# Longer transfer runs, another order for the first batch and narrower key sums in a sketched attention with a multiplicative FFN

## The chip, the core and the metric

The kernel runs on one core of one Trainium2 chip. A core has five engines that run side by side: TensorE (PE; its weight loads are shown as PEld), VectorE (DVE), ScalarE (ACT), GpSimd (POOL) and SyncE (SP), which here issues all transfers. The metric is the time of one execution in device microseconds.

## What is computed

Four batches, four heads, 1088 positions, head width 32. Queries and keys are sketched with two 8 x 32 matrices S1 and S2; the outer product of the two sketches is a feature vector of 64. Attention is linear in these features. Its output, as a 4352 x 128 matrix, goes through an FFN without a nonlinearity.

```python
def phi(x):
    a = np.einsum('rd,bhsd->bhsr', S1, x)
    b = np.einsum('rd,bhsd->bhsr', S2, x)
    return np.einsum('bhsi,bhsj->bhsij', a, b).reshape(*x.shape[:-1], r * r)
q_p, k_p = phi(q), phi(k)
kv = np.einsum('bhsf,bhsd->bhfd', k_p, v)
z = np.sum(k_p, axis=2)
num = np.einsum('bhsf,bhfd->bhsd', q_p, kv)
den = np.einsum('bhsf,bhf->bhs', q_p, z)[..., None] + 1e-06
x = (num / den)                    # then (B,H,S,D) -> (B*S, H*D)
a = x @ w1; b = x @ w2             # 4352 x 1024
out = ((a * b) @ w3) @ w_out       # 4352 x 128
```

q, k and v come as float32, S1, S2 and the weights as float64.

## The kernel before

**Layout.** A batch has 1024 "main" positions (128 partitions x 8 consecutive positions j) and a rest of 64; the rests of two batches share a tile. All four heads of a position lie side by side as 128 columns. `load_main` (L83-86) loads one tensor of one batch in four transfers, one per head, into a tile [128, 8, 4, 32]; the runs are one position of one head, 128 bytes.

**Keys** (`k_steps`, L408-479). `lead` (L389) rounds all of k to a coarse grid: k1 (bf16), the remainder k2 (DVE, L395) and ks = k + k1 (POOL, L396). For each half of four chunks of 128 positions, `k_feat` transposes k (L366), copies it (ACT, L368), multiplies it with the sketches (L375), copies one factor (L379) and forms the features kp (DVE, L383). Then `kvs` runs `gram` (L412) for each chunk: v' kp in two products, each for two heads (64 array columns, L415), k1' k1 (L418, bf16) and k2' ks (L419), both for all four heads at once (128 columns, of which the blocks of one head with itself are used). `fin1` to `fin4` (L439-478) add the rest, mask out the blocks, and turn the sums through two small chains of products into the operands Rh, Rf, Rl that the queries are multiplied with, and kz.

**Queries** (`q_steps`, L485-607), for each half of a batch: transposes (L498), a copy (L500), rounding on DVE into q1 and, with a subtraction on POOL (L508), q2; `ay`: for each chunk a bf16 product (L518) and two fp32 ones (L523, L525); then `split`, `dens` and `phi`, all DVE; transposes of the features (L584), a copy (L587), the product with kz (L602) and a copy to xT (L605), the FFN's input.

**FFN.** There are nine groups, eight of 512 positions (half a batch) and the rest of 256. In `ffn_ab` each group runs eight steps c: a (L646), a copy of a on ACT (L648), b (L650), and a*b on DVE (L652). w3 and w_out are multiplied on chip into w3o; `ffn_o` (L659) multiplies each a*b with it, LAG = 10 steps behind `ffn_ab`. `ffn_out` transposes and stores.

**Weights.** Each chunk of 128 x 512 float64 words arrives raw, up to NRAW = 6 at a time, and `convert` (L199-217) makes float32 of it with two ACT operations (L209, L210) and four of DVE (L212 to L216). There are 4 chunks of w1 and w2, 2 of w_out and 16 of w3; those of w3 are transposed (L327) and multiplied with w_out (L335).

**Order.** Each part is a list of steps with a cost; `merge` (L694) interleaves lists in proportion to their costs, and L712-726 write the stages down: first the keys and queries of batch 0 with the conversion of w1 and w2, then FFN group 0 with the next half of the queries and half of the remaining conversions, and so on. The framework's planner takes this order as a priority: where an engine would be idle by its own model, it puts in an instruction that comes later in the program but is ready. All transfers wait in SP's one queue in the order so planned.

## Time and profile before

| | us |
|---|---|
| median of three runs | 360.63 (360.4 to 361.77) |
| the profiled execution | 360.9 |
| its span | 359.1 |
| busy: PE, PEld, DVE, ACT, POOL | 309.2, 182.1, 207.1, 115.4, 22.3 |
| DMA packets (20.70 MB) | 58643, of which 53760 under 512 B |

The profile is of one execution. A row of a timeline or chain gives start and length in us, the engine, the line of the kernel, and the tile that is written; "x8" means that eight instructions are merged in the row. An fp32 product is two instructions, each with a weight load of its own. A group row gives the busy time, the mean of one instruction in ns, and the idle time in front of them. Windows give the busy time of each engine in a stretch. SPq is the issue of transfers on SP. The granted clock is the share of TensorE's full clock that its throttle passes on.

### The profile page before, as it was taken

The numbers are of one execution on the slowest core, as the hardware profiler recorded it, in microseconds if no ns is written. First come the engines' busy times: TensorE is split into PE (matmuls) and PEld (weight loads), VectorE is DVE, ScalarE is ACT, GpSimd is POOL, SyncE is SP. The second block draws the span as 40 slices with busy tenths as digits, with TensorE's granted clock in tenths as the row PEclk, the third lists the DMA queues.
The fourth block names the chain that finished last, engine by engine and source line by source line (L and its number), as shares of the span: only waits on it lengthen the run. The fifth ranks groups of instructions, "written<-read, shape, count | busy, mean of one in ns | idle before, by whom it ended". The sixth has DMA issues, their size and how long they took to land.

```text
span 359.1 us, 4019 instructions
## 1 busy us (share of the span) xinstructions
PE 309.2 (86%) x1404; PEld 182.1 (51%) x1404; DVE 207.1 (58%) x575; ACT 115.4 (32%) x211; POOL 22.3 (6%) x21
## 2 busy tenths in 40 slices
PE   2488224299999999999999999999999999999993
PEld 1354214237666766746554544655454454354652
DVE  6655977948994696637654573743348364362210
ACT  1144024245793323242222224130322422333311
POOL 0300021010000020001030101000010100000000
PEclk9995555559999999999999999999999999999998
DMA  7899699146300330012000000000000000000001
GB/s 102 143 320 130 132 187 379 55 70 226 117 0 2 58 60 1 0 24 37 31 0 0 0 33 0 0 31 0 0 2 29 1 0 31 0 29 0 3 28 44
DMA packets 58643, 20.70 MB, mean 58 GB/s; under 512 B 53760, under 2 KB 55040, under 8 KB 58624
## 3 DMA queue, kind: packets, MB, share of 16 engines
q1 hardware_dynamic: 58624, 20.46, 25.4%
q8 instruction: 11, 0.18, 0.2%
q14 instruction: 8, 0.07, 0.1%
HBM read 18.22 MB, written 2.23 MB: 57 GB/s over the span
## 4 chain that ended last, share of the span: by engine, by line
PE 80%; DVE 9%; SPq 3%; ACT 2%; DMA 2%; POOL 1%; issue 1%; DVEq 0%; POOLq 0%; ACTq 0%
PE ps_o L659 16%; PE a_ps L646 16%; PE b_ps L650 15%; PE ps_kvz L415 4%; PE ps_w3o L335 4%; PE ps_kvz L419 3%; PE ps_ay L523 3%; PE ps_x L602 3%; PE ps_ay L525 3%; PE ps_ph L584 2%; PE ps_ab L375 2%; SPq L85 2%; PE ps_wt L327 2%; PE ps_kvz L418 2%; DMA k_sb<-in_k_dram 2%; POOL q L508 1%
## 5 line engine op out<-in xcount | busy, mean ns | idle before, releaser
L652 DVE TENSOR_TENSOR ab<-ffa,b_ps 128x512 f32<-128x512 f32 (+1 forms) x72 | 47.2, 655 | 56.8 <-PE b_ps L650 52.8
L646 PE MATMUL a_ps<-xT,w 128*128 128x512 f32 (+1 forms) x144 | 72.6, 587 | 0.0
L650 PE MATMUL b_ps<-xT,w 128*128 128x512 f32 (+1 forms) x144 | 71.3, 577 | 0.0
L659 PE MATMUL ps_o<-ab,w3o 128*128 128x512 f32 (+1 forms) x144 | 69.4, 578 | 0.7 <-ACT ob L662 0.7
L648 ACT COPY ffa<-a_ps 128x512 f32<-128x512 f32 (+1 forms) x72 | 40.5, 562 | 82.9 <-PE a_ps L646 82.9
L650 PEld LDWEIGHTS b_ps<-xT,w 128*128 128x128 f32 x144 | 27.2, 193 | 28.2 <-issue 25.1
L659 PEld LDWEIGHTS ps_o<-ab,w3o 128*128 128x128 f32 x144 | 25.5, 190 | 24.7 <-issue 20.5
L646 PEld LDWEIGHTS a_ps<-xT,w 128*128 128x128 f32 x144 | 24.4, 195 | 14.9 <-issue 11.5
L508 POOL TENSOR_TENSOR q<-qT,q 128x512 f32<-128x512 f32 (+1 forms) x9 | 10.0, 1107 | 178.3 <-DVE q L232 178.3
L415 PE MATMUL ps_kvz<-kp,v_sb 128*64 128x128 f32 x128 | 16.2, 335 | 3.3 <-DVE kp L383 3.3
L419 PE MATMUL ps_kvz<-ks,k 128*128 128x128 f32 (+1 forms) x72 | 18.5, 344 | 0.0
L209 ACT ACTIVATE cv_c<-raw 128x512 f32<-128x512 f32 x22 | 14.7, 674 | 11.3 <-DVE cv_t L215 8.0
L523 PE MATMUL ps_ay<-Rf,q 128*128 128x64 f32 (+1 forms) x72 | 15.0, 301 | 3.4 <-POOL q L508 3.4
L224 DVE TENSOR_REDUCE g_q<-qT 128x1 f32<-128x512 f32 (+1 forms) x9 | 5.9, 657 | 20.0 <-ACT qT L500 20.0
L584 PE MATMUL ps_ph<-ident,ph 128*128 128x128 f32 x68 | 10.0, 290 | 8.7 <-DVE ph L577 8.7
L335 PEld LDWEIGHTS ps_w3o<-wo,w3T 128*128 128x128 f32 x128 | 15.6, 192 | 2.4 <-issue 2.4
L396 POOL TENSOR_TENSOR ks<-k_sb,k 128x1024 f32<-128x1024 f32 x4 | 10.6, 2651 | 95.2 <-DVE k L232 95.2
L335 PE MATMUL ps_w3o<-wo,w3T 128*128 128x128 f32 x128 | 16.3, 276 | 0.0
L215 DVE SCALAR_TENSOR_TENSOR cv_t<-cv_c,cv_t 128x512 int32<-128x512 int32 x22 | 15.8, 723 | 0.3
L210 ACT ACTIVATE cv_m<-raw 128x512 int32<-128x512 uint32 x22 | 14.7, 675 | 3.0 <-DVE w3c L216 2.6
L525 PE MATMUL ps_ay<-Rl,qT 128*128 128x96 f32 (+1 forms) x72 | 15.0, 302 | 0.0
L584 PEld LDWEIGHTS ps_ph<-ident,ph 128*128 128x128 f32 x68 | 8.6, 150 | 12.6 <-issue 12.3
(156 smaller groups left out, 386.9 us busy)
## 6 DMA issues: line engine op xcount, KB each, us to landing
raw<-in_moe_w_dram SPq DMA_DIRECT2D x20, 512.0 KB, 5.3
k_sb<-in_k_dram SPq DMA_DIRECT2D x16, 128.0 KB, 3.8
v_sb<-in_v_dram SPq DMA_DIRECT2D x16, 128.0 KB, 4.0
q_sb<-in_q_dram SPq DMA_DIRECT2D x16, 128.0 KB, 3.4
out_dram<-oT SPq DMA_DIRECT2D x8, 256.0 KB, 2.1
raw<-in_moe_w_out_dram SPq DMA_DIRECT2D x2, 512.0 KB, 9.1
kr<-in_k_dram SPq DMA_DIRECT2D x4, 32.0 KB, 2.3
vr<-in_v_dram SPq DMA_DIRECT2D x4, 32.0 KB, 2.3
```

The lines of the kernel that those rows point to most:

```text
L215: nc.vector.scalar_tensor_tensor(t, ci, -(1 << 31), t, ALU.bitwise_and, ALU.bitwise_or)
L335: nc.tensor.matmul(ps, t[:, c], wo[:, c], start=(c == 0), stop=(c == NC - 1))
L415: nc.tensor.matmul(acc["kv"][64 * p:64 * (p + 1)], vt[rows, 2 * p:2 * p + 2].rearrange("p h d -> p (h d)"), kp_chunk[rows, 2 * p:2 * p + 2 ...
L419: nc.tensor.matmul(acc["g2"], k2[rows], ks[rows], start=False, stop=last, skip_group_check=True)
L523: nc.tensor.matmul(C[rows, j, :64], s["q2"][:, cols], Rf[:, b].rearrange("p x h i -> p (x h i)"), start=True, stop=False, skip_group_check ...
L525: nc.tensor.matmul(C[rows, j], s["qT"][:, cols], Rl[:, b].rearrange("p x h i -> p (x h i)"), start=False, stop=True, skip_group_check=True)
L584: nc.tensor.transpose(ps[:, p, j * 128:(j + 1) * 128], s["ph"][:, j, 2 * p:2 * p + 2].rearrange("p h i j -> p (h i j)"), ident)
L646: nc.tensor.matmul(a_ps[:, :n], w1[:, cols], xT[key], start=True, stop=True)
L648: nc.scalar.copy(a_sb[:, :n], a_ps[:, :n])
L650: nc.tensor.matmul(b_ps[:, :n], w2[:, cols], xT[key], start=True, stop=True)
L652: nc.vector.tensor_mul(ab[:, :n], a_sb[:, :n], b_ps[:, :n])
L659: nc.tensor.matmul(o_ps[g][:, :n], w3o[:, c], ab_sb.pop((g, c))[:, :n], start=c == 0, stop=c == NC - 1)
```

## The change

1. **Transfers.** `load_main` becomes one transfer per tensor and batch, into a tile [128, 4, 8, 32]; a run is the eight positions of one head, 1 KB. The order "position, then head", which the transposes need, is made by a copy on ACT for each half (`natural`), for k and for q.
2. **First batch first.** The stage of batch 0 is an explicit order of steps instead of a merge: both halves' transposes and features come before the first sums; the query transposes and rounding come between the steps of the key chain; the four conversions of w1 and w2 are put at given places. The preparation of the sketches becomes three steps in it. The loads are issued k, its rest, v, q, then weights. For batch 0, ks is formed on DVE instead of POOL, and the keys use the three PSUM buffers of tag "h".
3. **Key sums** in products of one head each, 32 array columns: for each chunk four products v' kp with 64 moving columns, four k2' ks and four k1' k1 with 32 each. All v' kp of a half come first, then all k2' ks, then all k1' k1. What follows in `fin1` works on 128 x 32 instead of 128 x 128 and spreads the result over the blocks at the end.
4. **Last product later.** `ffn_o` runs 16 steps behind in groups 0 and 1, is then brought down to 4 behind in a stage of its own beside the first query half of batch 1, and stays 6 behind later and 2 in the last group.
5. **Smaller ones.** In `ay`, the bf16 products of all four chunks come first. `convert` uses the target as its scratch tile, and NRAW is 4. Four spreads of the sketches go from DVE to POOL. A one-element ACT copy is put at the start.

The core of the diff:

```diff
-LAG = 10
-NRAW = 6
+LAG = 16
+NRAW = 4
...
     def load_main(t, src, b):
-        for h in range(H):
-            nc.sync.dma_start(t[:, :, h], bass.AP(tensor=src.tensor, offset=(b * H + h) * S * D,
-                                                  ap=[[NJ * D, 128], [D, NJ], [1, D]]))
+        nc.sync.dma_start(t.rearrange("p h j d -> p h (j d)"),
+                          bass.AP(tensor=src.tensor, offset=b * H * S * D,
+                                  ap=[[NJ * D, 128], [S * D, H], [1, NJ * D]]))
...
+    def natural(t, half):
+        n = work.tile([128, 4, H, D], F32, tag="nat", name="nat")
+        nc.scalar.copy(n, bview(t[:, 0, 4 * half], [[D, 4], [NJ * D, H], [1, D]]))
+        return n.rearrange("p j h d -> p j (h d)")
...
-    load_k(0)
+    load_in("k", 0)
     load_rest(k_rs[0], k, 0)
+    load_in("v", 0)
+    load_in("q", 0)
     load_rest(v_rs[0], v, 0)
-    load_q(0)
     load_raw(NRAW)
...
-    def lead(kf, n, pool, name):
+    def lead(kf, pool, name, eng):
...
-        nc.gpsimd.tensor_add(ks, kf, k1)
+        def second():
+            nc.vector.tensor_sub(k2, kf, k1)
+            eng.tensor_add(ks, kf, k1)
...
-            for p in range(2):
-                nc.tensor.matmul(acc["kv"][64 * p:64 * (p + 1)], vt[rows, 2 * p:2 * p + 2].rearrange("p h d -> p (h d)"),
-                                 kp_chunk[rows, 2 * p:2 * p + 2].rearrange("s h i j -> s (h i j)"),
-                                 start=first, stop=last, skip_group_check=True)
-            nc.tensor.matmul(acc["g1"], k1[rows], k1[rows], start=False, stop=last, skip_group_check=True)
-            nc.tensor.matmul(acc["g2"], k2[rows], ks[rows], start=False, stop=last, skip_group_check=True)
+            def products(out, lhs, rhs, start):
+                for i, c in enumerate(chunks):
+                    for h in range(H):
+                        nc.tensor.matmul(out[h * D:(h + 1) * D], c[lhs][rows, h], c[rhs][rows, h],
+                                         start=start and i == 0, stop=last and i == len(chunks) - 1,
+                                         skip_group_check=True)
+            products(acc["kv"], "v", "kp", first)
+            products(acc["g2"], "k2", "ks", False)
+            products(acc["g1"], "k1", "k1", False)
...
-    run(merge(rest_steps(0) + k_steps(0) + q_main(0, 0), weight_steps(("w1", "w2"))))
-    w_st = weight_steps(("wo", "w3"))
-    cut = len(w_st) // 2
-    run(merge(ffn_steps(0), q_main(0, 1), w_st[:cut]))
-    run(merge(ffn_steps(1), k_steps(1) + q_main(1, 0), w_st[cut:]))
-    run(merge(ffn_steps(2), q_main(1, 1), rest_steps(1) + k_steps(2)))
...
+    w_in, w_out = weight_steps(("w1", "w2")), weight_steps(("wo", "w3"))
+    (ld1, ld2, tr0, ab0, kv0, tr1, ab1, kv1, *fins), r0, q00 = ([f for _, f in x] for x in (k_steps(0), rest_steps(0), q_main(0, 0)))
+    wi = [f for _, f in w_in]
+    for f in ([sketch_pairs, tr0, tr1, sketch_T, ld1, ab0, ld2, ab1] + r0 + [kv0, kv1, fins[0], sketch_P, q00[0], fins[1], q00[1],
+              wi[0], fins[2], fins[3], wi[1], q00[2], wi[2]] + q00[3:5] + [wi[3]] + q00[5:]):
+        f()
+    cut = len(w_out) * 2 // 5
+    run(merge(ffn_steps(0, 16), q_main(0, 1), w_out[:cut]))
+    run(merge(ffn_steps(1, 16), k_steps(1), w_out[cut:]))
+    run(merge(ffn_steps(None, 4), q_main(1, 0)))
+    run(merge(ffn_steps(2, 6), q_main(1, 1), rest_steps(1) + k_steps(2)))
...
```

In the explicit order, `q00[0]` are the query transposes, `q00[1]` their rounding, `q00[2]` the products, `q00[3:5]` `split` and `dens`, and `q00[5:]` the rest up to xT; `fins` are `fin1` to `fin4`, and `wi` the four conversions of w1 and w2.

More of the change, by code (lines that the diff above doesn't have):

```diff
@@ L410, in k_steps, with gram, ld1, chunk @@
         acc = {}
-        def gram(k1, k2, ks, kp_chunk, vt, rows, first, last):
-            k1, k2, ks = (x.rearrange("p h d -> p (h d)") for x in (k1, k2, ks))
-            for p in range(2):
-                nc.tensor.matmul(acc["kv"][64 * p:64 * (p + 1)], vt[rows, 2 * p:2 * p + 2].rearrange("p h d -> p (h d)"),
-                                 kp_chunk[rows, 2 * p:2 * p + 2].rearrange("s h i j -> s (h i j)"),
-                                 start=first, stop=last, skip_group_check=True)
-            nc.tensor.matmul(acc["g1"], k1[rows], k1[rows], start=False, stop=last, skip_group_check=True)
-            nc.tensor.matmul(acc["g2"], k2[rows], ks[rows], start=False, stop=last, skip_group_check=True)
-        def ld():
-            acc["k"] = lead(k_sb[b], NJ * HD, work, "")
-        st.append((1.0, ld))
+        def gram(chunks, rows, first, last):
+            def products(out, lhs, rhs, start):
[7 more added lines that the diff above has]
+            products(acc["g1"], "k1", "k1", False)
+        def ld1():
+            acc["k"], first, acc["second"] = lead(k_sb[b], work, "", nc.gpsimd if b else nc.vector)
+            first()
+        st += [(0.5, ld1), (0.5, lambda: acc["second"]())]
         for half in range(NJ // 4):
-            feat, state = k_feat(lambda j, half=half: k_sb[b][:, 4 * half + j].rearrange("p h d -> p (h d)"), 4, None)
+            def chunk(half=half):
+                n = natural(k_sb[b], half)
+                return [n[:, j] for j in range(4)]
+            feat, state = k_feat(chunk, 4, None, "t" if b else "h")
             st += feat
@@ L610, in srcs @@
         def srcs():
-            return [q_sb[b][:, 4 * half + j].rearrange("p h d -> p (h d)") for j in range(4)]
+            n = natural(q_sb[b], half)
+            return [n[:, j] for j in range(4)]
         def after():
             if half == 1 and b + 2 < B:
-                load_q(b + 2)
+                load_in("q", b + 2)
         return q_steps(srcs, (b, half), [[(b, 0, 128)]] * 4, after)
```

236 lines of the change are left out of this document (121 added, 115 removed).

## The prediction

> **What bounds the kernel now.** I read the windows first, cut at the places where the matrix engine's work changes: the first FFN product starts at 75.24 us, the last piece of w3 @ w_out and the second FFN group are done by 158.65, the last group's products end near 345.5.
>
> ```profile
> 0.00:75.24 75.24, 34.73 (x154) 24.88 (x155) 53.62 (x175) 21.74 (x38) 8.23 (x11) 0.69 0.82 173
> 75.24:158.65 83.41, 82.31 (x450) 53.35 (x450) 58.03 (x141) 37.41 (x70) 4.44 (x3) 0.97 0.25 58
> 158.65:345.50 186.85, 184.80 (x775) 99.33 (x774) 95.04 (x258) 54.12 (x99) 9.65 (x7) 1.00 0.05 13
> 345.50:359.10 13.60, 7.38 (x29) 4.52 (x28) 0.42 (x1) 2.10 (x5) 0.00 (x0) 0.90 0.10 29
> ```
>
> The columns are length, then busy time of PE, PEld, DVE, ACT and POOL, the granted clock, the DMA share and GB/s. From 75.24 to 345.50 PE is busy for 267.1 of 270.3 us: that part only gets shorter if PE gets less to do. Before 75.24 PE is busy for less than half, at a clock of 0.69 on average, and that part gets shorter if the chain of the first batch does. The chain of waits shows this chain (start, length, what; an excerpt without holes of its longest pieces):
>
> ```profile
> 13.63 1.13 PE ps_kt L366 x4
> 15.42 1.98 PE ps_ab L375 x8
> 17.73 1.24 DVE kp L383
> 27.75 1.15 DVE kp L383
> 40.78 1.14 DVE g_k L224
> 42.65 5.75 DMA k_sb<-in_k_dram
> 50.52 1.13 PE ps_qt L498 x4
> 54.29 1.21 POOL q L508
> 60.90 1.12 DVE g_k L224
> 68.42 1.95 PE ps_ph L584 x8
> 70.39 1.02 ACT pT L587
> 71.46 2.00 PE ps_x L602 x4
> 74.12 1.11 PE ps_qt L498 x4
> 75.24 1.71 PE a_ps L646 x2
> ```
>
> Three things stand out. The second half of the keys gets its features (27.75) ten microseconds after the first (17.73), because PE runs the first half's sums in between. Work of the next batch lies on the chain (g_k at 40.78 and 60.90, the k_sb transfer at 42.65), because the planner fills DVE with whatever is ready. And the queries are transposed at 50.52, when everything of the keys is done. The same windows over the two stretches in which DVE carries the chain, and DVE's largest groups in each (line, what | busy us, mean ns | idle):
>
> ```profile
> 36.00:49.60 13.60, 3.04 (x12) 2.78 (x12) 13.02 (x43) 0.00 (x0) 2.12 (x1) 0.50 0.85 157
> 59.79:75.24 15.45, 5.03 (x17) 2.98 (x18) 13.60 (x38) 5.30 (x8) 0.00 (x0) 0.50 0.28 113
> ```
>
> ```profile
> L395 DVE TENSOR_TENSOR k<-k_sb,k 128x1024 f32<-128x1024 f32 x1 | 2.9, 2894 | 0.0
> L216 DVE CUSTOM_DVE_ANT_0 wo<-cv_t,cv_m 128x1024 uint16<-128x1024 uint16 x2 | 1.4, 693 | 0.1
> L215 DVE SCALAR_TENSOR_TENSOR cv_t<-cv_c,cv_t 128x512 int32<-128x512 int32 x2 | 1.4, 680 | 0.0
> L224 DVE TENSOR_REDUCE g_k<-k_sb 128x1 f32<-128x1024 f32 x1 | 1.2, 1207 | 0.0
> ```
>
> ```profile
> L215 DVE SCALAR_TENSOR_TENSOR cv_t<-cv_c,cv_t 128x512 int32<-128x512 int32 x4 | 2.7, 684 | 0.0
> L212 DVE TENSOR_SCALAR cv_c<-cv_c 128x512 f32<-128x512 f32 x6 | 2.4, 422 | 1.6 <-ACT cv_c L209 1.6
> ```
>
> All of these rows are foreign to the first batch's chain: at least 6.9 us (2.9 + 1.4 + 1.4 + 1.2) in the first stretch and, with g_k's 1.12, at least 6.2 us (2.7 + 2.4 + 1.12) in the second.
>
> **Part 1: the first batch's chain.** I move five marks of the chain, before to after.
>
> *Mark 1, first transposes of the keys: 13.63.*
>
> ```profile
> 1.54 3.05 SPq L85 DMA_DIRECT2D k_sb<-in_k_dram  x4
> ```
>
> ```profile
> raw<-in_moe_w_dram SPq DMA_DIRECT2D x20, 512.0 KB, 5.3
> k_sb<-in_k_dram SPq DMA_DIRECT2D x16, 128.0 KB, 3.8
> ```
>
> The four pieces of k are issued from 1.54 to 4.59, and a piece lands 3.8 us after its issue; then the small rest rows go first on PE and DVE. After, one issue at 1.54 brings all 512 KB. A raw chunk is as large and lands in 5.3 us with longer runs and other transfers in front of it; that is the upper bound, a piece's 3.8 the lower: 5.3 to 6.8, I take 6.0, the middle. New is the reordering copy (natural, 128x512 on ACT). The kT copy has that shape, and with its hand-over lasts from 14.76 (13.63 + 1.13) to 15.42: 0.66. Mark 1 becomes 6.7. Sixteen such copies are 10.6 us of ACT, which is busy for 115 of 359; they need only landed data and two buffers, so the planner can put them early; if one is not, PE waits 0.66 us for it, at most 13 times, in the stall term below.
>
> *Mark 2, sums over the keys done.* Two rows of the key sums at the slow clock (the main chunk at 33.08, the rest at 34.46), and two at full clock:
>
> ```profile
> 33.08 0.70 PE L415 MATMUL ps_kvz<-kp,v_sb 128*64 128x128 f32 x4
> ...
> 34.46 0.69 PE L415 MATMUL ps_kvz<-kpr,vr 64*64 64x128 f32 x4
> ```
>
> ```profile
> 169.57 0.44 PE L415 MATMUL ps_kvz<-kp,v_sb 128*64 128x128 f32 x4
> ...
> 170.38 0.44 PE L415 MATMUL ps_kvz<-kp,v_sb 128*64 128x128 f32 x4
> ```
>
> A chunk of 128 positions takes 1.38 us slow and 0.81 at full clock; a batch has eight and the rest. So mark 2 is 34.46 + 1.38 = 35.8. After, a chunk is 8 + 8 + 4 = 20 matrix instructions with their loads, each of 32 array columns, instead of 4 + 1 + 2 = 7. What such a pair costs, no row shows. The nearest ones:
>
> ```profile
> 330.54 0.69 PE L602 MATMUL ps_x<-pT,kz 128*64 128x64 f32 x16
> 331.15 0.70 PE L659 MATMUL ps_o<-ab,w3o 128*128 128x512 f32 x1
> ```
>
> ```profile
> 85.74 1.78 PE ps_w3o L335 x16
> ```
>
> Sixteen pairs of 64 columns, in two column groups, take 0.61 us, 38 ns each; sixteen of 128 columns take 1.78, 111 ns each. If the load goes by its columns, 32 of them cost 111/4 = 28 ns. I take 32 ns, between 28 and 38, since the first row is the only one with column groups: 0.64 us a chunk at full clock. For the slow clock I take 1.0, between 0.64 (issue sets the pace) and 1.28 (array does). The Trainium skill (TensorEngine Tiling (Array Packing), Instruction Overhead) speaks against narrow products: some 60 cycles for each however short, so one should not divide a dimension that is small already. By its figure and the 2.4 GHz clock it gives, a pair would be estimated at 25 ns and a chunk at 0.50 us; the sum would be 3.8 us lower; no row here shows the floor itself.
>
> After mark 1: transposes 1.13, copy 0.66, products 1.98, a copy of b with hand-over 0.33 (15.42 + 1.98 to 17.73), kp 1.24: the sums start at 6.7 + 5.3 = 12.0. The second half's transposes and products now stand ahead of the first half's sums, so its kp ends 1.3 us later, inside the first four chunks. The split of k (ks now on DVE for this batch) runs beside the transposes and products. Nine chunks of 1.0: mark 2 becomes 21.0.
>
> *Mark 3, operands of the queries ready: 49.6, 13.8 us later.* Of DVE's 13.02 us at least 6.9 are foreign, so the way itself is at most 6.9 of these. Conversions and the next batch's split stay to be done and will still be fitted in: I take 12.0, nearer to what was seen. 33.0.
>
> *Mark 4, first query products done: 59.8, 10.2 us later.* Query transposes, their rounding and POOL's difference move ahead, under the key chain's waits. What is left is the stretch from POOL's end (54.29 + 1.21 = 55.5) to 59.8: 4.3. If the cover fails it is 10.2. 37.3.
>
> *Mark 5, first FFN product: 75.24, 15.4 us later.* At least 6.2 foreign. One conversion (w2's last) is put in by hand; I take 13.2, bounds 9.2 and 15.4. 50.5.
>
> So the FFN starts 75.2 − 50.5 = **24.7 us earlier**. With the bounds of all marks it lies between 37 and 60 (5.3 + 0.66 + 5.3 + 5.8 + 6.9 + 4.3 + 9.2 = 37; 6.8 + 0.66 + 5.3 + 11.5 + 13.8 + 10.2 + 15.4 = 64, of which 60 if the early queries hide at least half).
>
> **Part 2: behind it.** *Key sums:* three batches of nine chunks, 27 × (0.81 − 0.64) = **4.6 us less** (27 × 0.05 = 1.4 to 27 × 0.25 = 6.8). *Query products:* the four bf16 products now run while POOL still works.
>
> ```profile
> PE ps_ay L523 <- POOL q L508: 3.4, 4, 1.1
> ```
>
> Four waits, 3.4 us in all, of which three more short products hide about a third: **1 us less** (0 to 3.4). *Transfers, 1 KB runs:* behind 75 us DMA is busy at 0.25 and less, so this is worth nothing more there. SP has fewer issues (12 instead of 48 for q, k, v). *Small moves:* the four spreads of the sketch to POOL, the masks of the key sums on 32 columns instead of 128, ACT's first copy pulled forward, four raw weight chunks in flight instead of six (5.3/4 = 1.3 us each, faster than DVE converts them): each is under 1 us of an engine that waits at that place, nothing. *Lag 16, then 6 or 2:* the same products in another order. Their cover is that FFN products need no w3 until the queue has to be emptied; what it costs is a stall if DVE is late. *Stalls:* DVE has 53.62 + 58.03 = 111.7 us to do by the 158.65 mark, and that mark would come near 132 us (158.65 − 24.7 − 1.5), of which the first 6 give DVE little: 89% of what is left, where it was busy for 70% of the second stretch. PE had 1.1 us of holes there; I add **6 us** (0 to 12), for this and for late reordering copies.
>
> **The sum.** The profiled execution took 360.9 us (span 359.1). 360.9 − 24.7 − 4.6 − 1.0 + 6 = 336.6; the median of the runs shown is 360.63, 0.3 lower: **336 us**.
>
> **The rivals.**
> - *DVE takes over.* The w3 conversions (some 1.8 us of DVE each in the three operations shown: 0.4 + 0.68 + 0.69) pile up behind the earlier start. For: DVE's 0.96 and 0.88 busy share in the two stretches. Against: PE has products that need no w3. If DVE reaches only 80% before the mark at 158.65, 111.7 us need 140 + 6, while my sum puts that mark at 158.65 − 24.7 − 1.5 + 6 = 138: 8 us more, 344.
> - *The planner keeps its order.* Foreign work stays on the chain and the queries' lead is not covered: stretches of 13.8, 10.2 and 15.4 behind mark 2, FFN at 60.4, with fewer stalls (2): 360.9 − 14.8 − 4.6 − 1 + 2 = 342.5. For: it is what the chain shows now.
> - *Pairs at the sequencer's pace.* Twenty pairs for seven: at some 60 ns, between the rows of 38 and 111, the 36 chunks cost 36 × 20 × 0.028 = 20 us more, 356. For it speaks only that no row has 32 columns. The Trainium skill (TensorE: Matmul & The Clock Gate, "Wait — 56ns, not 53.3ns?") names about 62 ns per product where the sequencer's program decodes it, which would make 358; the 38 ns row speaks against that path here.
> - *Slower: narrow products do not overlap.* A pair of 32 columns costs what a full one does, 111 ns: 36 × 20 × 0.079 = 57 us more, 393. It decides against the change from 67 ns a pair (32 + 25 us / 720 pairs). For: twenty loads per chunk. Against: the 16 pairs at 38 ns, which overlapped.
> - *Nothing comes of it:* the first batch's gain returns wholly as DVE stalls. The engine's 70% speaks against.
>
> **How the numbers follow.** Forecast 0.56, with a range of its own from 322 to 346; DVE 0.19; planner 0.14; pairs at 60 ns 0.05; slower 0.05; nothing 0.01. Differences under 0.5% (1.8 us) can't be told from none here. Faster 0.56 + 0.19 + 0.14 + 0.05 = 0.94, same 0.01, slower 0.05. Low end: FFN at 43 and 2 us of stalls and 6.8 from the sums, 322; below that lies what a chain free of foreign work would give. High end: the DVE and planner rivals with some 7 us for both partly together, 351. Outside remain the two rivals on pairs and the tails.
>
> **What would show it.** The first a_ps near 50 us and key transposes near 7; both kp within 2 us of each other; a key chunk near 0.64 us at full clock (batch 1 to 3), no more than 1.0 in the first; PE's busy share over 95% from the first FFN product on; DVE over 80% in the 80 us behind it. I am wrong in part 1 if the FFN starts after 57, in part 2 if a pair takes over 40 ns or PE has over 12 us of holes behind the start.

## The result and the profile after

The changed kernel takes 325.87 us (median; 325.37 to 326.37) where the kernel before took 360.51 in the same session: a ratio of 0.903, 95% interval 0.901 to 0.906, 34.6 us less. The profiled execution took 325.53 us, its span is 323.7. The forecast was 336 with a range from 322 to 351: the direction and the likeliest case came true, the size was 10 us short.

The windows of the changed kernel, cut at the first FFN product, at the end of the last piece of w3 @ w_out and at 309 us, with the columns of the first fence of the prediction. Only the first cut falls on the same work as before: the last group's a and b go on to 315.9 here, and to 345.5 in the kernel before.

```profile
0.00:54.47 54.47, 24.16 (x271) 20.57 (x272) 47.27 (x150) 22.48 (x41) 8.63 (x14) 0.72 0.73 228
54.47:118.20 63.73, 62.04 (x505) 42.56 (x505) 53.25 (x126) 37.47 (x72) 4.33 (x2) 0.97 0.29 93
118.20:309.00 190.80, 188.46 (x1057) 98.49 (x1057) 100.03 (x277) 60.13 (x111) 10.77 (x8) 1.00 0.03 11
309.00:323.70 14.70, 8.78 (x43) 7.14 (x42) 2.53 (x6) 3.18 (x9) 0.00 (x0) 0.89 0.09 27
```

Two parts of the gain can be read off. The first FFN product comes at 54.47 instead of 75.24, 20.8 us earlier. And from there to the end of the span it takes 269.2 us (323.7 − 54.47) instead of 283.9 (359.1 − 75.24), 14.6 less. That second part is work, not waiting: PE is busy for 259.3 us behind the FFN's start (62.04 + 188.46 + 8.78) instead of 274.5, while its idle time there is 9.9 us (269.2 − 259.3) instead of 9.4.

Where the 14.6 come from shows in the key sums. One half batch (four chunks; 80 pairs of a weight load and a product) at full clock, an excerpt of PE's timeline:

```profile
150.23 0.65 PE L428 MATMUL ps_kvz<-kp,v_sb 128*32 128x64 f32 x32
150.70 0.45 PE L428 MATMUL ps_kvz<-ks,k 128*32 128x32 f32 x30
...
151.20 0.66 PE L374 MATMUL ps_kt<-ident,nat 128*128 128x128 f32 x4
```

From 150.23 to 151.20 it is 0.97 us, 12 ns a pair: the v' kp pairs 14.7 ns (0.47 / 32), the k2' ks pairs about 8.5 (0.27 / 32). A chunk takes 0.24 us; it took 0.81 before and the forecast was 0.64. A batch with its rest takes 2.3 us (0.97 + 0.97 + 0.32) instead of 7.1 (3.14 + 3.14 + 0.80, to the next product of something else), so three batches give 14.4.

The chain of the first batch (start, length, what; again an excerpt of its main pieces):

```profile
4.11 6.28 DMA q_sb<-in_q_dram
10.46 0.63 ACT nat L105
11.13 1.12 PE ps_qt L523 x4
12.25 3.32 PE ps_ab L383 x16
...
16.87 3.43 PE ps_kvz L428 x177
...
30.10 1.12 DVE g_k L231
...
34.39 1.20 DVE k L407
35.59 2.27 DVE cv_c L214
...
47.64 1.96 PE ps_ph L606 x8
49.62 1.02 ACT pT L609
50.69 2.00 PE ps_x L624 x4
52.71 0.59 ACT xT L627
53.35 1.12 PE ps_qt L523 x4
54.47 1.71 PE a_ps L669 x2
```

The five marks of the prediction, forecast and measured: first key transposes 6.7 and 6.3; key sums done 21.0 and 20.3; operands of the queries 33.0 and 33.4; first query products done 37.3 and 37.8; FFN 50.5 and 54.5. Four of them are within 0.7 us. But the second one is met by two misses that cancel: the sums start at 16.9 and not at 12.0, and last 3.4 us and not 9. What held their start is new: at the head of the chain stands the transfer of q, not of k. The queues of ACT and DVE show why:

```profile
7.44 0.58 ACT L376 COPY kT<-ps_kt 128x512 f32<-128x512 f32 x1 [0.75 <-PE ps_kt L374]
10.46 0.62 ACT L105 COPY nat<-q_sb 128x512 f32<-128x512 f32 x1 [2.43 <-DMA q_sb<-in_q_dram]
10.98 0.58 ACT L376 COPY kT<-ps_kt 128x512 f32<-128x512 f32 x1
...
11.32 0.22 DVE L295 TENSOR_TENSOR S12blk<-ST,mask 128x64 f32<-128x64 f32 x1
```

The planner put the reordering copy of q between the two copies of the key transposes. It waits for q's transfer (4.11 + 6.28 = 10.39), and the second kT, whose transposes were done near 8.3, waits behind it. On PE the query transposes stand in front of the products with the sketches in the same way. And these products need S12blk, the sketches laid out in blocks, which DVE writes at 11.54 (11.32 + 0.22), behind the rounding of k. So two things hold them until about the same time.

The last miss is the stretch from 37.8 to 54.47, 16.7 us where 13.2 were forecast and 15.4 were taken before. Behind the features ph it takes 6.0 us, as before (48.51 to 54.47 here; 69.28 to 75.24 there), with the chain on PE and ACT. In front of them DVE carries the chain, for 10.7 us (37.8 to 48.51) instead of 9.5 (59.79 to 69.28), and without a hole. Some of its rows there:

```profile
42.02 0.68 DVE L217 SCALAR_TENSOR_TENSOR wo<-cv_c,wo 128x512 int32<-128x512 int32 x1
...
43.37 0.68 DVE L218 CUSTOM_DVE_ANT_0 wo<-wo,cv_m 128x1024 uint16<-128x1024 uint16 x1
...
45.75 0.62 DVE L217 SCALAR_TENSOR_TENSOR w3c<-cv_c,w3c 128x512 int32<-128x512 int32 x1
...
46.49 0.67 DVE L218 CUSTOM_DVE_ANT_0 w3c<-w3c,cv_m 128x1024 uint16<-128x1024 uint16 x1
47.09 1.42 DVE L599 TENSOR_TENSOR ph<-ay,bs 128x256 f32<-128x256 f32 x4
```

Twelve instructions in that stretch, 5.5 us from their starts to the next start, are conversions of w_out and w3, work for later. In the kernel before, five such instructions (2.4 us) and the maximum of the next keys (1.1) stood there. The earlier the first batch runs, the more of such work is ready to be fitted in between its steps.

### The profile page after: what moved, and what is told of

The parts are those of the page before. It is cut to its first block, busy times and chain, and to the rows that moved or that the text cites. A ratio compares the mean times of both kernels' runs of the same rounds, so it can differ in the third digit from the quotient of the medians.

```text
span 323.7 us, 4894 instructions
## 1 busy us (share of the span) xinstructions
PE 283.4 (88%) x1872; PEld 168.8 (52%) x1872; DVE 203.1 (63%) x559; ACT 123.3 (38%) x232; POOL 23.7 (7%) x24
## 4 chain that ended last, share of the span: by engine, by line
PE 77%; DVE 13%; ACT 2%; DMA 2%; issue 2%; POOL 1%; SPq 1%; DVEq 0%; POOLq 0%; ACTq 0%
PE ps_o L682 17%; PE a_ps L669 16%; PE b_ps L673 16%; PE ps_w3o L340 4%; PE ps_x L624 3%; PE ps_ab L383 3%; PE ps_kvz L428 3%; PE ps_ph L606 2%; PE ps_ay L547 2%; PE ps_ay L545 2%; DMA q_sb<-in_q_dram 2%; PE ps_wt L332 2%; POOL q L533 1%; PE ps_qt L523 1%; DVE ab L675 1%
## 5 line engine op out<-in xcount | busy, mean ns | idle before, releaser
L669 PE MATMUL a_ps<-xT,w 128*128 128x512 f32 (+1 forms) x144 | 71.8, 581 | 0.0
L682 PEld LDWEIGHTS ps_o<-ab,w3o 128*128 128x128 f32 x144 | 25.4, 190 | 26.2 <-issue 23.8
L669 PEld LDWEIGHTS a_ps<-xT,w 128*128 128x128 f32 x144 | 24.7, 194 | 15.0 <-issue 11.3
L533 POOL TENSOR_TENSOR q<-qT,q 128x512 f32<-128x512 f32 (+1 forms) x9 | 10.9, 1211 | 156.3 <-DVE q L237 156.3
L340 PEld LDWEIGHTS ps_w3o<-wo,w3T 128*128 128x128 f32 x128 | 15.4, 192 | 2.4 <-ACT w3T L334 1.2
L212 ACT ACTIVATE cv_m<-raw 128x512 int32<-128x512 uint32 x22 | 15.0, 680 | 4.4 <-DVE w L218 3.0
L606 PEld LDWEIGHTS ps_ph<-ident,ph 128*128 128x128 f32 x68 | 8.6, 150 | 14.4 <-issue 13.2
L545 PE MATMUL ps_ay<-Rf,q 128*128 128x64 f32 (+1 forms) x72 | 13.6, 281 | 2.2 <-POOL q L533 2.2
L408 POOL TENSOR_TENSOR ks<-k_sb,k 128x1024 f32<-128x1024 f32 x3 | 9.5, 3151 | 75.1 <-DVE k L237 62.0
L609 ACT COPY pT<-ps_ph 128x1024 f32<-128x1024 f32 (+1 forms) x9 | 8.7, 965 | 13.7 <-PE ps_ph L606 13.7
L559 DVE TENSOR_REDUCE g_ay<-ps_ay 128x32 f32<-128x256 f32 (+1 forms) x9 | 3.7, 408 | 15.8 <-PE ps_ay L547 15.8
L545 PEld LDWEIGHTS ps_ay<-Rf,q 128*128 128x128 f32 (+1 forms) x72 | 11.2, 201 | 3.5 <-POOL q L533 3.4
```

The costliest lines, as they stand in the source:

```text
L212: nc.scalar.mul(m, lo.bitcast(U32), 2.0 ** -29)
L340: nc.tensor.matmul(ps, t[:, c], wo[:, c], start=(c == 0), stop=(c == NC - 1))
L533: nc.gpsimd.tensor_sub(s["q2"], s["qT"], s["q1"])
L545: nc.tensor.matmul(C[rows, j, :64], s["q2"][:, cols], Rf[:, b].rearrange("p x h i -> p (x h i)"), start=True, stop=False, skip_group_check ...
L606: nc.tensor.transpose(ps[:, p, j * 128:(j + 1) * 128], s["ph"][:, j, 2 * p:2 * p + 2].rearrange("p h i j -> p (h i j)"), ident)
L669: nc.tensor.matmul(a_ps[:, :n], w1[:, cols], xT[key], start=True, stop=True)
```

## The experiments

Times are medians; ratios are to the kernel before in the same session. Differences between two changed kernels are of medians from different sessions, in which the kernel before took 360.5 to 361.1 us, so under 1 us they say little. The marks are first starts of the FFN's a (L669) in the timeline, where it is 75.03 before and 54.26 after.

**The narrow sums alone, in the kernel before.** `gram`, `kvs` and `fin1` of the change, everything else as before:

```diff
-            for p in range(2):
...
-            nc.tensor.matmul(acc["g1"], k1[rows], k1[rows], start=False, stop=last, skip_group_check=True)
-            nc.tensor.matmul(acc["g2"], k2[rows], ks[rows], start=False, stop=last, skip_group_check=True)
+            products(acc["kv"], "v", "kp", first)
+            products(acc["g2"], "k2", "ks", False)
+            products(acc["g1"], "k1", "k1", False)
```

> The kernel before with the narrow key sums alone (20 pairs of 32 columns per chunk, all else as before). In the trace of the changed kernel a half batch of such sums takes 0.98 us at full clock and the rest 0.33, where the wide ones take 3.24 and 0.81: 4.95 us less per batch. Theory (the narrow sums themselves give most of what lies behind the first FFN product): 3 x 4.95 = 15 behind it and up to 9 in the first batch at the slow clock, 336 to 346 us. Rival (what the change gained behind the first FFN product came from fewer holes in PE, by lag and order): the sums give what I forecast for them, about 5 and 3 us, 352 us or more.

343.63 us, ratio 0.952 (0.948 to 0.955), inside the theory's 336 to 346. So half of the change's gain, 17.4 us, comes from part 3 alone. The FFN starts 6.8 us earlier (68.20), and 10.6 us are gained behind it (359.1 − 75.03 = 284.1 before, 341.7 − 68.20 = 273.5 here), not the theory's 15: PE is busy for 12.1 us less behind the start (262.6 instead of 274.7) and idle for 1.5 us more. Why not more of the 14.4 arrives isn't shown.

**Short runs and wide sums in the changed kernel, and short runs alone.** Sums over 128 columns of four heads need the heads of a position side by side, and the 1 KB layout has them apart; so one run undoes parts 1 and 3 together and one undoes part 1, and the difference is part 3.

```diff
-        nc.sync.dma_start(t.rearrange("p h j d -> p h (j d)"),
-                          bass.AP(tensor=src.tensor, offset=b * H * S * D,
-                                  ap=[[NJ * D, 128], [S * D, H], [1, NJ * D]]))
+        for h in range(H):
+            nc.sync.dma_start(t[:, :, h], bass.AP(tensor=src.tensor, offset=(b * H + h) * S * D,
+                                                  ap=[[NJ * D, 128], [D, NJ], [1, D]]))
...
-                n = natural(k_sb[b], half)
-                return [n[:, j] for j in range(4)]
+                return [k_sb[b][:, 4 * half + j].rearrange("p h d -> p (h d)") for j in range(4)]
```

> The changed kernel with 128-byte runs (no reordering copy) and the wide key sums; order, lag and the rest stay. Theory: 15 us of the key sums come back behind the first FFN product, some 6 to 9 of them in the first batch, and 1 to 3 for the transfers: 347 to 353 us. Rival (order and lag carry the gain): at most 340 us.

> The changed kernel with four transfers of 128-byte runs for each of q, k, v and batch and without the reordering copy on ACT; narrow sums, order and lag stay. Theory (transfers matter only up to the first key transposes): the first transposes 1 to 4 us later, 326 to 330 us. Rival (the 1 KB runs carry the earlier start): the first FFN product 8 us later or more, 334 us or more.

349.95 us (0.969, 0.966 to 0.971) and 334.37 us (0.927, 0.922 to 0.932). With short runs in both, the narrow sums are worth 15.6 us beside the other parts too. Part 1 is worth 8.5 us (334.37 − 325.87), where the prediction gave it a little in front of mark 1 and nothing behind; the theory's 326 to 330 is missed, and the rival's time came without its 8 us in front of the FFN, which starts 5.2 us later (59.42). SP's queue in the run with short runs, and then a row of PE:

```profile
16.59 8.54 SPq L85 DMA_DIRECT2D k_sb<-in_k_dram  x4
...
40.96 3.37 SPq L85 DMA_DIRECT2D v_sb<-in_v_dram  x4
44.43 1.45 SPq L136 DMA_DIRECT2D raw<-in_moe_w_out_dram  x2
```

```profile
25.12 0.69 PE L516 MATMUL ps_qt<-ident,q_sb 128*128 128x128 f32 x2 [2.21 <-issue]
```

The four issues of one tensor, 4096 runs of 128 bytes, take 2.7 to 4.2 us of SP and once 8.54. Of the 5.2 us, 1.4 are there at the first key transposes (7.74 instead of 6.32) and 1.6 at the end of the sums (21.86 instead of 20.29). Two more come from the queries: their transposes stand behind the sums here, with a hole of 2.21 us among them in which PE waits for nothing that the profile shows, and DVE waits 2.43 us for their copy; the query products start 3.7 us later (36.62 instead of 32.94). So not all of it is the transfers' own time.

The raw w_out is issued at 44.43 instead of 24.15, behind k, v and q of two batches and more, and lands at 50.66. Its conversion begins on ACT at 55.70, where in the change DVE has finished it by 44.1. The chain that the profile gives for this run passes through that transfer, but DVE has no idle time from 40.8 to 53.7 and no conversion of w_out among its rows there, so the transfer did not hold the features. The work that it delays falls behind the FFN's start, where PE is idle for 12.6 us instead of 9.9; that the one makes the other is argued, not shown.

**The same pairs, heads outside, chunks inside.** All products of one head (one column group of the array) come in a row, instead of the four groups in turn:

```diff
-                for i, c in enumerate(chunks):
-                    for h in range(H):
+                for h in range(H):
+                    for i, c in enumerate(chunks):
```

> The changed kernel with the two loops of the key sums exchanged: all products of one head, on one group of 32 array columns, follow each other, then the next head's. Same products, same number. Theory (the four column groups work at the same time, that is why a pair takes 8 to 15 ns): in one group a product of 64 columns in fp32 needs at least its own 53 ns, a chunk about 0.7 to 1.3 us instead of 0.25, so 12 to 28 us more in batches 1 to 3 and some 4 in the first: 342 to 358 us. Rival (a narrow pair is cheap by itself): within 2 us of 325.9.

332.68 us, ratio 0.921 (0.918 to 0.924): 6.8 us more than the change, between the rival's 328 and the theory's 342. PE's timeline of one half batch at full clock:

```profile
106.01 1.23 PE L428 MATMUL ps_kvz<-kp,v_sb 128*32 128x64 f32 x29
...
107.20 0.62 PE L428 MATMUL ps_kvz<-ks,k 128*32 128x32 f32 x23
...
107.94 1.13 PE L669 MATMUL a_ps<-xT,w 128*128 128x512 f32 x2
```

1.93 us instead of 0.97, 24 ns a pair instead of 12; the v' kp pairs take some 35 ns (1.01 / 29 until the next row), the k2' ks pairs some 19 (0.44 / 23). So taking the column groups in turn is worth a factor of two: 0.96 x 6 = 5.8 us behind the start, and 2.5 in the first batch, whose sums take 5.9 us instead of 3.4; of these 8.3 us 6.8 arrive at the end. The theory's floor of 53 ns for a product with 64 moving columns did not hold. And a pair is far below the 111 ns of a full-width one even so. With 128 columns loaded the moving ones make little difference, as a row of the kernel before shows, at full clock (0.83 us for 8 pairs with 64 moving columns, 104 ns each):

```profile
166.87 1.00 PE L375 MATMUL ps_ab<-S12blk,kT 128*128 128x64 f32 x8
167.70 1.08 PE L646 MATMUL a_ps<-xT,w 128*128 128x512 f32 x2
```

With 32 loaded and 64 moving a pair takes 35 ns, so it is the columns loaded that make the difference here; with 32 loaded the moving ones count too (35 and 19).

**The first stage merged as before.** The steps of batch 0 in `merge`, all else as changed:

```diff
-    for f in ([sketch_pairs, tr0, tr1, sketch_T, ld1, ab0, ld2, ab1] + r0 + [kv0, kv1, fins[0], sketch_P, q00[0], fins[1], q00[1],
-              wi[0], fins[2], fins[3], wi[1], q00[2], wi[2]] + q00[3:5] + [wi[3]] + q00[5:]):
-        f()
+    for f in (sketch_pairs, sketch_T, sketch_P):
+        f()
+    run(merge(rest_steps(0) + k_steps(0) + q_main(0, 0), w_in))
```

> The changed kernel with the first stage merged in proportion to costs, as before (sketches first, then the rest of the keys, keys, queries of batch 0, with w1 and w2 between them), instead of the explicit order. Theory (the explicit order is worth what puts the second half's features ahead of the first sums and the queries under the key chain): first FFN product 4 to 9 us later, 330 to 335 us. Rival (with short sums the planner finds as good an order): within 2 us of 325.9.

335.87 us, ratio 0.931 (0.929 to 0.933): the written order is worth 10.0 us, and the FFN's start moves by 10.9, to 65.19, both a little beyond the theory's 335 and 9.

**Lag and stages of before.**

```diff
-    run(merge(ffn_steps(0, 16), q_main(0, 1), w_out[:cut]))
-    run(merge(ffn_steps(1, 16), k_steps(1), w_out[cut:]))
-    run(merge(ffn_steps(None, 4), q_main(1, 0)))
...
+    run(merge(ffn_steps(0, 10), q_main(0, 1), w_out[:cut]))
+    run(merge(ffn_steps(1, 10), k_steps(1) + q_main(1, 0), w_out[cut:]))
...
```

> The changed kernel with the stages and the lag of before behind the first stage (10 steps throughout, half of the conversions beside group 0, the queries of batch 1 in the stage of group 1). Theory (PE has no holes that the lag closes; the same products in another order): 325 to 328 us. Rival (the longer lag hides late conversions on DVE): over 330 us, with PE holes before the last product of w3 and w_out.

327.16 us (0.906, 0.904 to 0.909): 1.3 us, inside the theory's 325 to 328. The interval overlaps the change's 0.901 to 0.906, so even this 1.3 isn't clear of noise.

**Query products alternating.** The bf16 product and the two fp32 ones of each chunk in turn, as before:

```diff
-            for b, j, rows, cols in spans:
-                nc.tensor.matmul(A[rows, j], s["q1"][:, cols], Rh[:, b].rearrange("p x h i -> p (x h i)"),
-                                 start=True, stop=True)
-            for b, j, rows, cols in spans:
...
+            for j, part in enumerate(parts):
+                for (b, c0, nn) in part:
...
```

> The changed kernel with the bf16 and fp32 products of the queries alternating chunk by chunk, as before. In the trace a set of four chunks takes 1.96 us with the bf16 products first and 2.29 when alternating. Theory: 0.33 us for each of eight sets behind the start and 1 us of waits for POOL, 328 to 330 us. Rival (the order only moves the waits): within 0.5 us of 325.9.

327.45 us (0.908, 0.906 to 0.910): 1.6 us, between both expectations. In this run's trace a set of four chunks takes 2.12 us (143.41 to 145.53) against 1.96 in the change (143.33 to 145.29). The 2.29 that the theory took from the kernel before holds a wait of 0.17; other sets there take 2.12 as well. The waits for POOL are 2.4 us here and 2.2 in the change.

**Products of the sums issued twice.** Each sum over the keys is doubled by it.

```diff
+            end = last
+            for last in (False, end):
                 products(acc["kv"], "v", "kp", first)
                 products(acc["g2"], "k2", "ks", False)
                 products(acc["g1"], "k1", "k1", False)
+                first = False
```

> The changed kernel with every product of the key sums issued twice (each sum over the keys is doubled by it). Theory: a pair costs 9 to 15 ns, a half batch 0.98 us at full clock, a batch 2.3 us with its rest, 3.4 to 3.8 us in the first batch: 3 x 2.3 + 3.5 = 10.4 us more, 336.3 us (334 to 338), and a half batch takes 1.95 us. Rival: a pair costs the 32 ns of the forecast and the gain behind the FFN's start came from fewer waits: 36 chunks x 20 x 0.032 = 23 us more, 349 us (345 to 353).

339.89 us (0.940, 0.938 to 0.942), 14 us more, above the theory's 334 to 338 and below the rival's 345. The price of a pair is as the theory has it: a doubled half batch takes 1.82 us, from 101.57 to 103.39.

```profile
101.57 0.65 PE L428 MATMUL ps_kvz<-kp,v_sb 128*32 128x64 f32 x32
...
103.39 0.66 PE L332 MATMUL ps_wt<-ident,w3c 128*128 128x128 f32 x4
```

What it had not foreseen are two holes in the first batch, in which PE waited for nothing that the profile shows:

```profile
22.56 0.33 PE L428 MATMUL ps_kvz<-kp,v_sb 128*32 128x64 f32 x3 [2.73 <-issue]
...
27.66 0.24 PE L428 MATMUL ps_kvz<-k 128*32 128x32 bf16 x6 [2.77 <-issue]
```

They are 5.5 us of the 9.5 by which the FFN starts later (63.8). The groups of PE between the two holes (instructions | us, mean ns | idle):

```profile
L428 PE MATMUL ps_kvz<-kp,v_sb 128*32 128x64 f32 x38 | 1.6, 311 | 2.7 <-issue 2.7
L428 PE MATMUL ps_kvz<-ks,k 128*32 128x32 f32 x64 | 1.6, 244 | 0.0
L428 PE MATMUL ps_kvz<-k 128*32 128x32 bf16 x26 | 0.8, 197 | 0.0
```

38 + 64 + 26 = 128 products with 128 loads: 256 instructions from hole to hole. More on this below.

**DVE cleared in front of the FFN.** The conversions of w_out and w3 and the key steps of batch 1 are queued behind the last feature product of the first query half:

```diff
-                nc.vector.tensor_mul(ph[:, j], bview(a, [[r, H], [1, r], [0, r]]), bview(b, [[r, H], [0, r], [1, r]]))
+                phi_last[0] = nc.vector.tensor_mul(ph[:, j], bview(a, [[r, H], [1, r], [0, r]]), bview(b, [[r, H], [0, r], [1, r]]))
...
+    def behind(steps):
+        def held(f):
+            def g():
+                with tc.issue_after(phi_last[1].ins):
+                    f()
+            return g
+        return [(c, held(f)) for c, f in steps]
...
+    phi_last[1] = phi_last[0]
+    w_out = behind(w_out)
...
-    run(merge(ffn_steps(1, 16), k_steps(1), w_out[cut:]))
+    run(merge(ffn_steps(1, 16), behind(k_steps(1)), w_out[cut:]))
```

> The changed kernel in which DVE's part of the conversions of w_out and w3 and of the keys of batch 1 is queued on DVE behind the last feature product of the first query half, so that the first batch's chain has DVE for itself. Theory (work of later stages, some 8 us in DVE between the key operands and the features, delays the first FFN product): first FFN product at 46 to 49 instead of 54.5 us and, PE being bound behind it, 319 to 323 us. Rival (what is pushed back is missing later): the start is as early, but PE gets 5 us or more of holes before w3 is done, 325 us or more.

322.75 us (0.894, 0.892 to 0.896), the fastest kernel of this study; a second time:

> The run with the conversions of w_out and w3 and the keys of batch 1 behind the last features of the first query half, once more, as the partner of the next run. Theory and rival both expect the 322.75 us of the first time within 0.6.

323.71 us (0.895, 0.893 to 0.897), 1.0 us above the first time and so outside the 0.6 expected, though the ratios agree. Against the change's 0.903 it is 2 to 3 us faster. Of its chain:

```profile
35.39 0.49 PE ps_ay L548 x2
...
41.74 1.95 PE ps_ph L607 x8
...
48.56 1.71 PE a_ps L670 x2
```

From the end of the query products (35.9) to the FFN it takes 12.7 us instead of 16.7, and the FFN starts 5.9 us earlier. In front of the features DVE now takes 6.7 us (35.9 to 42.6) instead of 10.7. Some 40% of the 5.9 is given back: from the FFN's start to the end the span has 271.8 us (320.1 − 48.35) instead of 269.4.

**The first batch's queues in another order.** Two runs on top of that one try to bring the key sums to the forecast 12.0. The first puts only DVE in order: the rounding of k and of its rest behind S12blk.

```diff
-        nc.vector.tensor_mul(S12blk, bview(ST, [[0, H], [r, 2], [1, r]]), bview(mask4, [[1, H], [0, 2], [0, r]]))
+        sk_last[0] = nc.vector.tensor_mul(S12blk, bview(ST, [[0, H], [r, 2], [1, r]]), bview(mask4, [[1, H], [0, 2], [0, r]]))
...
+    ld1, ld2 = (f for _, f in behind([(0, ld1), (0, ld2)], sk_last, 0))
+    r0[:2] = (f for _, f in behind([(0, f) for f in r0[:2]], sk_last, 0))
```

> On top of that, the rounding of k and of its rest is queued on DVE behind the sketch's last step (S12blk). Theory: in the changed kernel the key sums start at 16.8 and not at the 12.0 forecast because S12blk was late, 11.3 to 11.5, behind k's maximum, rounding and remainder on DVE. With S12blk near 7 the first products with the sketches start near 8.5 instead of 11.9; the rounding (1.2 + 0.8 + 1.2 + 1.2 us) now ends near 11.6 and the two kp behind it near 14, so the sums start near 14 instead of 16.6. The FFN starts 2 to 2.6 us earlier (near 46), about half comes back behind: 320.5 to 322.0 us. Rival: the rounding was as late itself, kp and ks only change places and the sums start at 16 or later: 322.3 to 323.5 us.

326.92 us (0.905, 0.903 to 0.906): slower than without, beyond what even the rival expected. S12blk was there at 9.3, and nothing came of it (PE's timeline):

```profile
11.29 0.69 PE L526 MATMUL ps_qt<-ident,nat 128*128 128x128 f32 x2 [2.49 <-ACT nat L105]
11.77 3.52 PE L385 MATMUL ps_ab<-S12blk,kT 128*128 128x64 f32 x16
...
20.28 0.66 PE L430 MATMUL ps_kvz<-ks,k 128*32 128x32 f32 x32 [1.25 <-DVE g_k L226]
```

The products with the sketches still start at 11.8, behind query transposes that wait for the copy of q; and ks, now behind both kp, comes at 20.2. So S12blk alone did not hold them. The second run keeps ks ahead of kp, has S12blk early too, and moves q out of the way on PE and ACT. Its marks are the sketch's spread (`sk_last`), S12blk (`S_last`), the last product of the keys with the sketches (`ab_last`; in the order of the program that is the rest's, not the second half's), its copy of b (`b_last`) and the rest's remainder (`k2_last`):

```diff
+    (_, ld1), = behind([(0, ld1)], sk_last, 0)
+    (_, ld2), = behind([(0, ld2)], S_last, 0)
+    (_, q00[0]), = behind(behind([(0, q00[0])], ab_last, 0), b_last, 0)
+    (_, wi[0]), = behind(behind([(0, wi[0])], k2_last, 0), b_last, 0)
+    q01[:1] = behind(q01[:1], b_last, 0)
```

> The run with the cleared DVE queue, and beside it three orders in the first batch: k's rounding behind the sketch's spread and ks behind S12blk on DVE; the query transposes behind the second half's key products on PE; on ACT the reordering copies of q and the first conversion behind the second half's copy of b. Theory, from the run before: what holds the key sums until 16.6 is the queue on ACT and PE. The reordering copy of q waits there for q's transfer (4.1 + 6.3 = 10.4 us), and behind it stand the kT copy of the second half on ACT and, behind the query transposes on PE, the 16 products with the sketches (11.9 to 12.3). With q out of the way these start near 9.4, when S12blk is there; the sums start near 13 and end near 17 instead of 20; the FFN starts 2 to 3.5 us earlier (45 to 46.5) and about half comes back behind: 320 to 322.3 us. Rival: the first batch is held by DVE whatever the order (conversions, rounding): the sums start at 15.5 or later, or the gain is lost before the FFN's start: 322.5 us or more.

325.07 us (0.899, 0.897 to 0.901): 1.4 us slower than the run with DVE cleared, which the rival expects, though the mechanism is the theory's:

```profile
9.43 3.65 PE L385 MATMUL ps_ab<-S12blk,kT 128*128 128x64 f32 x16 [0.63 <-DVE S12blk L297]
...
14.32 1.08 PE L430 MATMUL ps_kvz<-kp,v_sb 128*32 128x64 f32 x32
...
22.07 0.48 PE L526 MATMUL ps_qt<-ident,nat 128*128 128x128 f32 x1 [2.85 <-issue]
...
34.13 0.37 PE L545 MATMUL ps_ay<-Rh,q 128*128 128x64 bf16 x4 [2.65 <-DVE Rh L497]
```

The products with the sketches start at 9.43, as the theory says, now behind S12blk. With S12blk early and q still in the way they started at 11.8, so q held them too; with q out of the way alone, S12blk at 11.54 would have held them, though no run has that. The sums start at 14.32 and end at 18.0, 2 us and more before those of the change (20.3) and of the two runs with DVE cleared. But the query products start at 34.13, later than the 31.9 and 32.7 of those two: the query transposes now come last, a hole of 2.85 us falls into them, and DVE, which waits 3.48 us for their copy before it goes on with the key chain at 23.8, has the rounding of q at 27.0 between that chain's steps (18.3 in the run with DVE cleared). A mark brought forward is worth only what the next queue lets through.

## Why the prediction came out as it did

**Part 1, the first batch (forecast 24.7 us earlier, measured 20.8).** Mark 1 was right (6.7 and 6.3). The written order carries this part, 10.9 us of the FFN's start when undone; short runs cost 5.2 of it. Three steps failed.
- *Mark 2's start.* "The sums start at 6.7 + 5.3 = 12.0" moved the chain's own pieces and forgot the queues that the reordering copies and the query transposes were put into. The prediction priced a late copy at 0.66 us; what it cost was the wait for q's transfer, which put the second kT off from 8.3 to 10.98. It gave S12blk no time, which DVE had ready only at 11.54. The run with both put right took 2.5 us of the 4.9 back (14.3 instead of 16.8).
- *Mark 2's length.* Nine chunks of 1.0 were taken, the 180 products lasted 3.4 us, 0.38 a chunk. That is 5.6 us less than forecast and by chance about as much as the start was late, so mark 2 came out at 20.3 by luck.
- *Mark 5.* The last stretch was taken to become 2.2 us shorter; it became 1.3 longer, 16.7 against 15.4. Only 3 of the 6.2 us that the prediction called foreign there stood in front of the features (two of the four rows of L215, one of the six of L212, and g_k); the others ran behind 69.28, when the chain was on PE and ACT, and could not shorten it. The run that queues the later work behind the first features takes 4 of the 16.7 away.

The rival in which the planner keeps its order had stretches of 13.8, 10.2 and 15.4 behind mark 2. The first and the last of them came as in that rival (13.1 and 16.7), the middle one as in the forecast (4.4).

**Part 2, behind the FFN's start (forecast 0.4 us more, −4.6 − 1 + 6; measured 14.6 less).** This is where the 10 us of error are.
- *The price of a narrow pair* is the term that was mis-sized: 32 ns, from the bounds 28 to 38, where 12 were measured; 14.4 us instead of 4.6. The step that failed is the pair of ends. "If the load goes by its columns, 32 of them cost 111/4 = 28 ns" is near the 24 ns that the pairs take when one group follows itself. What it left out is that four column groups in turn halve this; the row with 38 ns has two groups, and 64 columns loaded. The rivals with 60 and 111 ns are out by the same row, and the run with all pairs doubled gives the price a second time (0.85 us more for 80 pairs). By its figure of some 60 cycles for each product, at the 2.4 GHz that the prediction took, the Trainium skill (TensorEngine Tiling (Array Packing), Instruction Overhead) gave an estimate of 25 ns a pair; the trace does not agree, as 80 pairs in 0.97 us lie at half of that.
- *Stalls*, 6 us forecast: PE's idle time behind the start grew by 0.5 us (9.4 to 9.9). DVE was busy for 84% of the second window (53.25 of 63.73) but for 76% of the 80 us behind the start (61.08 us), under the 80% that was the sign for stalls. The prediction's own argument against the rival, that PE has products that need no w3, fits this. The rival in which DVE takes over is out. That the cover is thin shows in the run with the cleared DVE, where 2.4 us come back.
- *Query products*, 1 us forecast: 1.6 us in the run that undoes their order, but not by the forecast's wait. The waits for POOL are 2.2 and 2.4 us there, and the rest fits the sets of products, 0.16 us shorter each.
- *Transfers, nothing forecast behind 75 us:* 8.5 us in all, of which 5.2 fall before the FFN's start and some 3 behind. The prediction went by the shares and packets of the page (0.25 busy) and did not follow SP's one queue, in which short runs put the raw w_out 20 us later.
- *Lag*, nothing forecast: 1.3 us, not clear of noise.

In numbers, the forecast of 336.6 goes with the measured start (+3.9) and pairs (−9.8) to 330.7; the profiled execution took 325.5. The 5.2 us between are what is left over: stalls and query products together were forecast at 5 us more and came out at 0.2 less (14.6 − 14.4). Undone one at a time the parts give 15.6 + 10.0 + 8.5 + 1.6 + 1.3 = 37 us, a little more than the 34.6 of the whole; they may share waits of the first batch.

What stays open: whether the holes of 2.7 us can be moved away from the first batch, and what kernel has both the early sums and the early queries. No run here has both.

## What to carry to other kernels

A product that computes blocks nobody needs is to be priced by what it loads and by what it streams: twenty narrow pairs, in the four column groups in turn, cost 0.3 of the seven wide ones here, and a price between two rows of other shapes missed that by a factor of 2.7. When a step is moved forward, follow every helper that it brings along into the queue of its own engine, and ask which transfer the first of them waits for: one copy of q, put ahead of the second copy of k, held the key sums, together with an operand that was late as well, by some 2.5 us; putting only the operand right gave nothing back. An earlier chain is filled with work that has become ready; put that work behind a mark of the chain, and expect a part of the gain to be lost later. And count work as foreign only where its engine carries the chain: half of what was counted in the last stretch here cost the chain nothing.

## What the runs showed of the hardware

- Pairs of weight load and product of 32 array columns go out every 8.5 to 15 ns when the four column groups alternate (32 moving columns 8.5, 64 moving columns 14.7), and every 19 to 35 ns when one group follows itself.
- PE seems to run out of program. With the sums doubled it stood twice for 2.7 us, with exactly 256 instructions in between, and in a kernel with an earlier front once for 2.85. In each of these three holes one packet of the instruction queue falls, of 16 KB. It begins 0.2 to 0.5 us behind the hole's beginning (20.01, 25.34 and 19.52) and lasts 1.0 to 1.2 us, and the hole ends 1.4 us behind the packet's end. The hole of 2.21 us in the run with short runs holds one too, begun 0.1 us in front of it. The instruction queue's transfers rise from 14 in the change to 20 with the doubled sums, which are 1440 more instructions (4 batches of 9 chunks of 40): 5.6 blocks of 256. The queue's row (transfers, MB, share) of both pages, the change first:

```profile
q8 instruction: 14, 0.23, 0.3%
```

```profile
q8 instruction: 20, 0.33, 0.4%
```

  From the end of the first hole to the end of the second it takes 5.1 us; two later holes of this kind last 0.6 and 0.8. The Trainium skill (Runtime: NRT & Kernel Launch, Instruction fetch mechanics) has a refill in blocks of 256 instructions and calls its cost mostly hidden, since instructions are dispatched more slowly than blocks arrive; the block's size agrees with the trace, and in these holes the cost is not hidden. This fits a PE that waits for a block whose packet moves only about when PE stops; why it does not move earlier isn't shown. The packet itself is no slower than those behind 100 us, which take 0.9 to 1.4 us, so nothing here says that other transfers slow it.
- Four issues of one 512 KB tensor in 128-byte runs kept SP for 2.7 to 4.2 us, and for 8.54 once; the one issue of the same tensor in 1 KB runs took 0.4 to 0.6, and once, behind 10 us, 2.8.
